# Causal attention with decay ahead of a two-layer MLP: a 32-row mask, wide transposes, and two blocks of pairs moved beside the first MLP block

## The chip, the cores and the metric

The kernel runs on one NeuronCore of a Trainium2 chip. The metric is the device time of one execution in microseconds (us), the median of several runs; less is better. TensorE (PE) multiplies matrices, VectorE (DVE), ScalarE (ACT) and GpSimd (POOL) work on elements, SyncE (SP) issues most of the transfers. Each engine takes its instructions in the order in which the program lists them.

## The reference

```python
scores = scale * np.matmul(q, k.transpose(0, 1, 3, 2))      # 8 batches, 8 heads, 576 x 64
s_pos = np.maximum(s, 0.0)
cum = np.cumsum(s_pos, axis=-1)
bias = -(cum[:, :, :, None] - cum[:, :, None, :])
scores = np.where(causal, -1000000000.0, scores + np.minimum(bias, 0.0))
attn = softmax(scores)
x = np.matmul(attn, v) -> transposed to 4608 tokens x 512
h = x @ w_in                                                 # 512 x 2048
g = h * np.clip(h + 3.0, 0.0, 6.0) / 6.0
out = g @ w_out                                              # 2048 x 512
```

The inputs and the output are float32; the kernel multiplies in float16.

## The kernel before

**Attention.** The 64 heads are taken as 32 pairs, four pairs to a batch. For each pair, `load_qk` and `load_v` bring q, k and v to SBUF in float32, in rows of 64 elements (256 bytes). `cast_qk` turns q and k to float16 on POOL, and `transpose_group` transposes them on TensorE in two halves of five and four tiles, with copies by DVE into `qkT`, whose halves are called `qT` and `kT`. There are three slots of `qkT`, `v_f`, `v_h` and `Pm`, and a pair p uses slot p % 3. From pair 10 on (`PTD`) the transposition is done by DMA (`cast_columns`, `transpose_dma`).

Rows 0 to 63 of `qT` and `kT` are q and k. Rows 64 to 67 add the decay: `kT` gets the running sum of s, split into three float16 parts (`kaug`), and `qT` gets its negative (`qaug`). A chain of DVE operations (`s8`, `c8`, `kaug`, L102 to L115) makes them for all heads. Pair 0 gets its rows from SBUF, the others from copies of `kaug` and `qaug` in DRAM (`load_aug`). Rows 68 to 127 are a coarse causal mask in steps of `GRAN` = 10 positions: a 1 in one operand meets -16384 in the other. It is copied from `amask` by ACT and DVE (`mask_rows`).

`scores_bank` multiplies one of four banks of scores, ACT takes the exponential into `Pm`, and POOL zeroes the upper triangle of the diagonal tiles (L295, four instructions a head). `attend` multiplies by v, with a column of ones that gives the row sums; DVE divides (L341, L343) into `xs`; `x_transpose` writes `xT`, the MLP's input.

**MLP.** The 4608 tokens are 9 blocks of 512. `m1(n, f)` is one of 16 column tiles of layer 1 (L408, four matmuls, then ACT's L416 and DVE's L417), `m2(n, t4, part)` a quarter of a row tile of layer 2 (L430). Weights come by casting DMAs from POOL: `load_w_in` in halves, `load_w_out` in quarters. Part p of layer 2 needs quarter p.

**Order.** The schedule is manual: an engine's order is that of the program. `att_tasks(p)` lists the steps of pair p; `att_of` groups them. The pairs 0 to 3 and the first part of pair 4 run alone. `weave` then deals attention tasks between MLP tasks in proportion to their costs: pairs 4 to 8 beside layer 1 of block 0 and the first eight tasks of layer 2, pairs 9 to 12 beside layer 1 of block 1 and the other eight, later four pairs beside each block. `loads` and `casts` within a pair's tasks issue later pairs' loads and casts; `pairs_at` and `weights_at` say which.

PSUM has eight banks: two of tag M, three of tag S, two of tag O, one of tag Y.

Of the kernel before, what the change touches and what calls it, by code (L numbers as in the profile page):

```python
# [9 lines left out]
F32 = mybir.dt.float32  # L10
# [6 lines left out]
def kernel(  # L17
# [23 lines left out]
    GRAN = 10  # L41
# [5 lines left out]
    NS = 3  # L47

# [3 lines left out]

    def bank():
        return psum.tile([128, 512], F32, tag="M", bufs=2, name="bank")

    ident_dram = nc.inline_tensor(np.eye(128, dtype=np.float16), name="ident_f16")

    gran = np.arange(SEQ) // GRAN
    rows = np.arange(60)
    amask_np = np.ones((2, 64, SEQ), dtype=np.float16)  # L60
    amask_np[0, 4:64] = gran[None, :] == rows[:, None]
    amask_np[1, 4:64] = np.where(gran[None, :] < rows[:, None], -16384.0, 0.0)
    amask_dram = nc.inline_tensor(amask_np, name="amask")

    row = np.arange(W2).reshape(NTR, 128).T % SEQ
    xaug_np = np.concatenate([amask_np[1][:, row], amask_np[0][:, row]], axis=2)
    xaug_dram = nc.inline_tensor(
        np.ascontiguousarray(xaug_np.transpose(1, 2, 0)).reshape(128, 2 * NTR * 64),
        name="xaug",
# [25 lines left out]
    amask = work.tile([128, 2, SEQ], F16, tag="amask", bufs=1)  # L95
    s_sb = work.tile([NH, SEQ], F32, tag="s0", bufs=1)
    nc.sync.dma_start(out=s_sb, in_=s.rearrange("b h t -> (b h) t"))
    nc.scalar.dma_start(out=amask[64:128], in_=amask_dram.ap().rearrange("i p t -> p i t"))
    nc.scalar.dma_start(out=ident, in_=ident_dram.ap())

# [18 lines left out]
    nc.gpsimd.memset(warm, 0.0)  # L119
    nc.gpsimd.memset(kT[:, :, W2:W2 + 64], 0.0)  # L120
    nc.gpsimd.memset(v_f[64:128, :, :, 4, :], 0.0)
    nc.gpsimd.memset(v_h[:, :, :, :, D:VW], 1.0)
    nc.gpsimd.memset(Pm[:, :, 1600:PW], 1.0)

    def mask_rows(sl, copy):
        for i, dst in enumerate((kT, qT)):
            copy(
                out=dst[64:128, sl, 0:W2].rearrange("p (h t) -> p h t", h=2),
                in_=amask[64:128, i:i + 1, :].to_broadcast([64, 2, SEQ]),
            )  # L130
# [5 lines left out]
    def load_qk(p, eng):  # L136
        b, h0 = (2 * p) // H, (2 * p) % H
        t = work.tile([128, NTR, 2, D], F32, tag="qkf", bufs=3, name=f"qkf{p}")
        for i, src in enumerate((q, k)):
            rows = src[b, h0:h0 + 2].rearrange("h s d -> (h s) d")  # L140
            eng.dma_start(  # L141
                out=t[:, :, i, :], in_=rows.rearrange("(t p) d -> p t d", p=128)
            )
        qk_f[p] = t

    def load_v(p, eng):
        b, h0 = (2 * p) // H, (2 * p) % H
        sl = p % NS
        for hh in range(2):
            eng.dma_start(  # L150
                out=v_f[:, sl, hh, 0:4, :],
                in_=v[b, h0 + hh, 0:512].rearrange("(t p) d -> p t d", p=128),
            )
        eng.dma_start(
            out=v_f[0:64, sl, :, 4, :],
# [9 lines left out]
    def cast_qk(p):  # L165
        t = work.tile([128, NTR, 2, D], F16, tag="qkh", bufs=2)
        nc.gpsimd.tensor_copy(out=t, in_=qk_f.pop(p))  # L167
        qk_h[p] = t

    xaug = cpool.tile([128, 2 * NTR, 64], F16, tag="c_xaug")  # L170

    def load_columns():
        nc.sync.dma_start(out=xaug.rearrange("p t c -> p (t c)"), in_=xaug_dram.ap())

    def copy_columns():
        for i in range(2):
            nc.vector.tensor_copy(out=xb[:, i, :, 64:128], in_=xaug)

# [47 lines left out]
    def cast_v(p):  # L226
        sl = p % NS
        copy = nc.vector.tensor_copy if p in (1, 2, 3, 4) else nc.gpsimd.tensor_copy
        copy(out=v_h[:, sl, :, :, 0:D], in_=v_f[:, sl])  # L229

    def half_bank(early):

        if early:
            return psum.tile([128, 640], F16, tag="M", bufs=2, name="pTm")
# [7 lines left out]
    def transpose_group(p, g):  # L242
        t0, t1 = ((0, 5), (5, 9))[g]
        n = (t1 - t0) * 128
        pT = half_bank(p < 5)
# [10 lines left out]


# [4 lines left out]
        (896, [(1, 256, 576), (4, 512, 576)]),  # L262
        (1280, [(2, 256, 576)]),
# [5 lines left out]
        (4, 4): 1216, (2, 2): 1280, (2, 3): 1408, (2, 4): 1536,  # L269
# [372 lines left out]
```

## Time and profile before

| | |
|---|---|
| median of 3 runs | 382.48 us (381.65 to 382.67) |
| span of the profiled execution | 378.1 us |
| busy, TensorE | 353.6 us (94%) |
| busy, VectorE / ScalarE / GpSimd | 190.8 / 210.4 / 146.4 us |
| first scores (L282) | 12.59 us |
| first matmul of layer 1 (L408) | 42.78 us |
| first matmul of layer 2 (L430) | 73.16 us |
| queue q1 (SP's transfers) | 182,536 packets, 54.52 MB, 68.2% of 16 engines |
| queue q0 (weights, from POOL) | 4.19 MB as written, 5.9% |

The span runs from the first to the last instruction of one profiled execution. A share of a queue is the time that its packets took, as a share of the span of all 16 DMA engines. A busy TensorE is not one at its peak, since matmuls overlap. In the listings, a row of the timeline gives start, duration, engine, line, operation, output and input, and in brackets how long the engine had been idle and what ended that.

### The profile page before, as it was taken

The numbers are of one execution on the slowest core, as the hardware profiler recorded it, in microseconds if no ns is written. First come the engines' busy times: TensorE is split into PE (matmuls) and PEld (weight loads), VectorE is DVE, ScalarE is ACT, GpSimd is POOL, SyncE is SP. The second block draws the span as 40 slices with busy tenths as digits, with TensorE's granted clock in tenths as the row PEclk, the third lists the DMA queues.
The fourth block names the chain that finished last, engine by engine and source line by source line (L and its number), as shares of the span: only waits on it lengthen the run. The fifth ranks groups of instructions, "written<-read, shape, count | busy, mean of one in ns | idle before, by whom it ended". The sixth has DMA issues, their size and how long they took to land.

```text
span 378.1 us, 7609 instructions
## 1 busy us (share of the span) xinstructions
PE 353.6 (94%) x2780; PEld 219.8 (58%) x2780; DVE 190.8 (50%) x329; ACT 210.4 (56%) x406; POOL 146.4 (39%) x375
## 2 busy tenths in 40 slices
PE   7766778899999999999999999999999999999995
PEld 3454455566666666666666666666666655555542
DVE  5554466875545444544444445445444554454531
ACT  4745466456866666666656666666666543443310
POOL 4365444364565444444444554454453100000000
PEclk9989699999999999999999999999999999999999
DMA  8699999945999999999999998999854001010011
GB/s 181 137 204 193 194 208 249 210 105 132 200 186 243 204 211 200 216 203 203 197 190 199 214 208 179 206 211 200 185 114 106 31 30 55 28 55 29 28 66 74
DMA packets 184621, 59.38 MB, mean 157 GB/s; under 512 B 177828, under 2 KB 178212, under 8 KB 184584
## 3 DMA queue, kind: packets, MB, share of 16 engines
q1 hardware_dynamic: 182536, 54.52, 68.2%
q0 software_dynamic: 1632, 4.19, 5.9%
q8 instruction: 22, 0.36, 0.4%
q10 hardware_dynamic: 416, 0.19, 0.2%
q14 instruction: 15, 0.12, 0.1%
HBM read 37.41 MB, written 9.73 MB: 125 GB/s over the span
## 4 chain that ended last, share of the span: by engine, by line
PE 82%; DMA 9%; DVE 3%; ACT 2%; SPq 1%; issue 1%; POOL 1%; POOLq 0%; ACTq 0%; DVEq 0%
PE bank L408 31%; PE po L430 30%; PE S L282 9%; PE O L331 7%; DMA qkf<-in_k_dram 5%; DMA v_f<-in_v_dram 3%; PE bank L430 3%; ACT Pm L290 2%; PE pT L369 1%; DMA s_sb<-in_s_dram 1%; PE bank L450 1%; SPq L141 1%; POOL t L167 1%; DVE qkT L253 1%; DVE kaug L115 0%
## 5 line engine op out<-in xcount | busy, mean ns | idle before, releaser
L416 ACT ACTIVATE trl<-bank,bias 128x512 f32<-128x512 f32 x144 | 99.5, 691 | 111.8 <-PE bank L408 110.8
L417 DVE SCALAR_TENSOR_TENSOR gT<-trl,bank 128x512 f16<-128x512 f32 x144 | 99.1, 688 | 121.8 <-ACT trl L416 121.8
L408 PE MATMUL bank<-xT,w_in 128*128 128x512 f16 x576 | 148.3, 383 | 1.3 <-DVE gT L417 1.3
L290 ACT ACTIVATE Pm<-S 128x384 f16<-128x384 f32 (+2 forms) x256 | 116.2, 505 | 32.3 <-PE S L282 30.6
L295 POOL TENSOR_SCALAR_AFFINE_SELECT Pm<-Pm 128x128 f16<-128x128 f16 (+2 forms) x256 | 79.0, 311 | 135.4 <-ACT Pm L290 126.6
L430 PE MATMUL po<-w_out_sb,gT 128*128 128x512 f16 x528 | 130.9, 379 | 0.0
L408 PEld LDWEIGHTS <-w_in 128*128 128x128 f16 x576 | 77.5, 146 | 31.6 <-issue 2.8
L430 PEld LDWEIGHTS <-gT 128*128 128x128 f16 x576 | 53.2, 98 | 51.4
L282 PE MATMUL S<-qkT 128*128 128x320 f16 (+4 forms) x448 | 70.2, 265 | 6.9 <-DVE qkT L253 2.3
L282 PEld LDWEIGHTS <-qkT 128*128 128x128 f16 x448 | 41.4, 99 | 34.2 <-DVE qkT L253 2.7
L331 PEld LDWEIGHTS <-Pm 128*128 128x128 f16 x960 | 39.1, 98 | 12.1 <-POOL Pm L295 0.4
L331 PE MATMUL O<-v_h,Pm 128*128 128x65 f16 x960 | 41.6, 195 | 0.3 <-POOL Pm L295 0.3
L343 DVE TENSOR_TENSOR xs<-O,r 128x640 f16<-128x640 f32 x32 | 26.4, 824 | 1.1
L213 POOL CAST xb<-qkf 128x1152 f16<-128x1152 f32 x22 | 25.3, 1149 | 0.0
L439 DVE TENSOR_SCALAR osb<-po 128x512 f32<-128x512 f32 x33 | 22.6, 685 | 5.0 <-PE po L430 5.0
L229 POOL CAST v_h<-v_f 128x640 f16<-128x640 f32 x28 | 20.6, 737 | 2.2 <-DMA v_f<-in_v_dram 2.2
L341 DVE RECIPROCAL r<-O 128x10 f32<-128x10 f32 x32 | 7.1, 220 | 25.6 <-PE O L331 25.4
L167 POOL CAST t<-qkf 128x1152 f16<-128x1152 f32 x10 | 11.8, 1177 | 12.2 <-DMA qkf<-in_k_dram 12.2
L238 PEld LDWEIGHTS <-t 128*128 128x128 f16 x90 | 6.3, 99 | 12.1 <-POOL t L167 8.2
L253 DVE COPY qkT<-pTm 64x640 f16<-64x640 f16 (+1 forms) x20 | 9.1, 453 | 7.8 <-PE pTm L238 7.6
L450 PE MATMUL bank<-warm 128*128 128x512 f16 x30 | 9.5, 487 | 2.2 <-POOL warm L119 1.4
L430 PE MATMUL bank<-w_out_sb,gT 128*128 128x512 f16 x48 | 11.3, 379 | 0.0
(40 smaller groups left out, 80.2 us busy)
## 6 DMA issues: line engine op xcount, KB each, us to landing
qkf<-in_q_dram SPq DMA_DIRECT2D x32, 288.0 KB, 3.6
qkf<-in_k_dram SPq DMA_DIRECT2D x32, 288.0 KB, 4.2
out_dram<-osb SPq DMA_DIRECT2D x36, 256.0 KB, 2.0
v_f<-in_v_dram SPq DMA_DIRECT2D x64, 128.0 KB, 3.6
w_in<-in_moe_w_in_dram POOLq DMA_DIRECT2D x2, 1024.0 KB, 11.0
w_out_sb<-in_moe_w_out_dram POOLq DMA_DIRECT2D x4, 512.0 KB, 8.3
v_f<-in_v_dram SPq DMA_DIRECT2D x32, 32.0 KB, 8.2
qkT<-xb SPq DMA_TRANSPOSE x22, 5.2
```

What stands on the lines that cost most here:

```text
L213: nc.gpsimd.tensor_copy(out=x.rearrange("p (i t) c -> p t i c", i=2)[:, :, :, 0:D], in_=qk_f.pop(p))
L229: copy(out=v_h[:, sl, :, :, 0:D], in_=v_f[:, sl])
L282: nc.tensor.matmul(out=S[:, c:c + hi - lo], lhsT=kT[:, sl, off + 128 * kt:off + 128 * (kt + 1)], rhs=qT[:, sl, off + lo:off + hi], start=( ...
L290: nc.scalar.activation(out=P[:, p0:p0 + n], in_=S[:, 0:n], func=AF.Exp, scale=0.125, bias=0.0)
L295: nc.gpsimd.affine_select(out=view, in_=view, pattern=pattern, compare_op=ALU.is_ge, fill=0.0, base=0, channel_multiplier=-1,)
L331: nc.tensor.matmul(out=O[:, hh, qt * VW:qt * VW + D + 1], lhsT=P[:, c:c + 128], rhs=v_h[:, sl, hh, kt, 0:D + 1], start=(qt == 0), stop=(qt ...
L343: nc.vector.tensor_tensor(out=xs.rearrange("p t h d -> p h t d"), in0=Ov[:, :, :, 0:D], in1=r.to_broadcast([128, 2, 5, D]), op=ALU.mult,)
L408: nc.tensor.matmul(out=ph, lhsT=w_in_t[f // 8][:, kc, f % 8, :], rhs=xT[:, kc, n * 512:(n + 1) * 512], start=(kc == 0), stop=(kc == KC - 1),)
L416: nc.scalar.activation(out=trl, in_=ph, func=AF.Relu, bias=bias3[:, 0:1], scale=1.0)
L417: nc.vector.scalar_tensor_tensor(out=gT[n][:, f, :], in0=trl, scalar=6.0, in1=ph, op0=ALU.min, op1=ALU.mult)
L430: nc.tensor.matmul(out=po, lhsT=gT[n][:, f, t4 * 128:(t4 + 1) * 128], rhs=w_out_sb[:, f, :], start=(f == 0), stop=(f == NF - 1),)
L439: nc.vector.tensor_scalar_mul(out=osb, in0=po, scalar1=1.0 / 6.0)
```

## The change

- The mask has 32 rows in steps of 18 (rows 68 to 99). Score matmuls read 100 rows (`KR`). The mask comes by DMA directly into `qkT`; DVE memsets write ones to rows 64 to 67 of all slots, and ones and zeros to the fixed columns of `xb`, ahead of the decay chain.
- q and k of pairs 0 and 1 (`ROWS`) are loaded in contiguous runs of nine rows per partition. Their transposes go to one tile of two banks (`transpose_rows`), and `rows_of_head` copies each head with strided reads. This pool is closed afterwards and its banks become those of tag M. Pair 0 is cast by ACT; v of pairs 0 and 1 is loaded by casting DMAs from POOL.
- A one-element copy by POOL, `hold`, waits for the end of the decay chain.
- Banks 2 and 3 of the scores are rearranged, so that three POOL instructions a head mask the diagonals.
- The order of the first two batches is written out by hand: pairs 0 to 3, then layer 1 of block 0 beside pairs 4 and 5, with three PSUM banks, then layer 2 of block 0 beside pairs 6 and 7. The first three tiles of layer 1 start with three of their four chunks. Pair 8 and what follows come after; layer 1 of block 1 has the last four tasks of layer 2 of block 0 beside it. w_in is loaded at the end of pair 0 and in pair 3, w_out in `own(5)`.

```diff
+    nc.vector.memset(qkT[64:68, :, 0:2 * W2], 1.0)
+    nc.vector.memset(xb[:, :, :, D:D + 4], 1.0)
+    nc.vector.memset(xb[:, :, :, KR:128], 0.0)
...
     def cast_qk(p):
         t = work.tile([128, NTR, 2, D], F16, tag="qkh", bufs=2)
-        nc.gpsimd.tensor_copy(out=t, in_=qk_f.pop(p))
+        if p == 0:
+            for i in range(2):
+                nc.scalar.copy(out=t[:, :, i, :], in_=qk_f[p][:, :, i, :])
+        else:
+            nc.gpsimd.tensor_copy(out=t, in_=qk_f[p])
+        qk_f.pop(p)
         qk_h[p] = t
...
+    load_v(0, nc.gpsimd)
+    load_v(1, nc.gpsimd)
...
+    def rows_of_head(p, hh):
+        for dst, r0 in ((kT, 64), (qT, 0)):
+            nc.vector.tensor_copy(
+                out=dst[0:64, p, hh * SEQ:(hh + 1) * SEQ].rearrange("d (j t) -> d j t", t=NTR),
+                in_=T_tiles[p][r0:r0 + 64, 0:W2].rearrange("d (t j) -> d j t", j=128)[
+                    :, hh * 64:(hh + 1) * 64
+                ],
+            )
...
-                lhsT=kT[:, sl, off + 128 * kt:off + 128 * (kt + 1)],
-                rhs=qT[:, sl, off + lo:off + hi],
+                lhsT=kT[0:KR, sl, off + 128 * kt:off + 128 * (kt + 1)],
+                rhs=qT[0:KR, sl, off + lo:off + hi],
...
-            if (n, t4) in ((0, 1), (8, 1), (8, 3)):
+            if (n, t4) in ((8, 1), (8, 3)):
...
+    load_qk(2, nc.sync)
     load_aug(1, nc.sync)
-    load_qk(2, nc.sync)
     load_v(2, nc.sync)
+    load_aug(2, nc.sync)
+    load_qk(3, nc.sync)
+    load_v(3, nc.sync)
...
+    def pair_of_first_batch(p):
+        s0, s1 = scores(2 * p), scores(2 * p + 1)
+        if p == 0:
+            return (
+                s0[:3] + step(transpose_rows, 1) + step(rows_of_head, 1, 0)
+                + step(rows_of_head, 1, 1) + step(single_banks) + s0[3:]
+                + s1 + step(cast_qk, 2) + step(load_w_in, 0) + att(0)
+                + step(load_aug, 3, nc.sync)
+            )
...
+    def own(p):
+        cast_qk(p)
+        if p == 5:
+            for c in range(4):
+                load_w_out(c)
+        cast_v(p)
+        load(p + 3)
...
+    def pair_of_next_batch(p):
+        s0, s1 = scores(2 * p), scores(2 * p + 1)
+        aug = step(load_aug, p + 3, nc.sync) if p + 3 < PTD else []
+        if p == 4:
+            return (
+                halves(4) + [(lambda: None, 1500)] + s0 + s1 + aug + att(8) + step(own, 5)
+            )
+        if p == 5:
+            return att(9) + halves(5) + xt(4) + [(lambda: None, 800)] + s0 + s1 + aug + att(10)
...
-    keep_warm(18)
-    cast_qk(0)
-    transpose_group(0, 0)
-    transpose_group(0, 1)
-    mask_rows(2, nc.vector.tensor_copy)
-    cast_v(0)
+    keep_warm(11)
+    transpose_rows(0)
+    rows_of_head(0, 0)
+    rows_of_head(0, 1)
+    nc.gpsimd.tensor_copy(out=hold, in_=kaug[:, 2, SEQ - 1:SEQ])
     cast_qk(1)
-    keep_warm(12)
-    for task, _ in att_of[0]:
+    load(4)
+    keep_warm(10)
+    for p in range(4):
+        for task, _ in pair_of_first_batch(p):
+            task()
+    x_transpose(2)
+    for f in range(2):
+        m1(0, f, range(3))
+    attend(7)
+    m1(0, 2, range(3))
+    x_transpose(3)
+    for f in range(3):
+        m1(0, f, range(3, 4))
+    m2_0 = m2_tasks(0)
+    m1_0 = m1_tasks(0)
+    own(4)
+    weave(pair_of_next_batch(4), m1_0[3:9])
+    weave(pair_of_next_batch(5), m1_0[9:])
+    own(6)
+    m2_0[0][0]()
+    attend(11)
+    load_columns()
+    decay_columns()
+    for task, _ in m2_0[1:4]:
         task()
+    x_transpose(5)
+    for task, _ in halves(6):
+        task()
+    m2_0[4][0]()
+    weave(att_of[1], m2_0[5:12])
+    weave(att_of[2], merged(m1_tasks(1), m2_0[12:], 1))
```

## The prediction

> **What bounds the kernel now.** I read the tenths of the page first, for where TensorE is not full.
>
> ```profile
> ## 2 busy tenths in 40 slices
> PE   7766778899999999999999999999999999999995
> ...
> PEclk9989699999999999999999999999999999999999
> DMA  8699999945999999999999998999854001010011
> ```
>
> A slice is 9.45 us. TensorE is full from slice 9 on; the eight slices before are not, and in most of those the DMA engines read 9. So the place to win time is the first 75 to 90 us, and the suspect there is the transfer of inputs. The table by stretches (span, busy us and count of each engine, granted clock, DMA share, GB/s), cut at 73.2 us, where layer 2 of block 0 begins, says how much is left to win:
>
> ```profile
> 0.00:73.20 73.20, 54.24 (x505) 35.55 (x506) 42.68 (x84) 40.45 (x78) 35.57 (x84) 0.93 0.96 196
> 73.20:121.20 48.00, 46.91 (x453) 30.96 (x453) 28.34 (x57) 30.43 (x64) 25.81 (x67) 1.00 0.85 173
> 121.20:373.70 252.50, 252.46 (x1829) 153.25 (x1826) 119.07 (x188) 139.49 (x264) 85.05 (x225) 1.00 0.68 144
> ```
>
> After 121.2 us TensorE is busy 252.46 of 252.50 us, and the waits of that stretch hold none for TensorE. The diff leaves that part's matmuls alone, so the end moves exactly as much as the moment from which TensorE is full. Third, the chain that ended last, in order of time (start, us, what), names what that moment waited for:
>
> ```profile
> 15.93 3.96 DMA qkf<-in_k_dram
> ...
> 27.48 11.71 DMA v_f<-in_v_dram
> 42.99 1.65 PE bank L408 x4
> ...
> 49.85 13.93 DMA qkf<-in_k_dram
> ...
> 73.23 0.97 PE po L430 x4
> ```
>
> Layer 1 starts at 43 us because the values of pair 4 took 11.7 us to land (both halves of w_in, issued at 26.3 and 30.8, were in flight), and layer 2 starts at 73.2 behind a key load of 13.9 us (all of w_out was in flight). Fourth, the timeline of the start (start, us, engine):
>
> ```profile
> 3.80 0.45 DVE L102 TENSOR_SCALAR s<-s_sb 64x576 f32<-64x576 f32 x1 [3.80 <-DMA s_sb<-in_s_dram]
> ...
> 7.42 1.58 DVE L115 TENSOR_TENSOR kaug<-r,kaug 64x576 f16<-64x576 f32 x1
> ...
> 12.59 0.71 PE L282 MATMUL S<-qkT 128*128 128x256 f16 x6
> ...
> 15.48 0.40 SPq L141 DMA_DIRECT2D qkf<-in_q_dram  x1
> ```
>
> The decay chain on VectorE (3.8 to 9.0) decides the first scores at 12.6: copies and the small row loads follow it. SP reaches pair 2 only at 15.5, since it queues behind the decay rows.
>
> **What the skill says.** (1) The Trainium skill, "DMA: Bandwidth & Descriptors", section "Queues, rings and completion order": each DMA engine goes round-robin between the queues that have work. The trace agrees: a quarter of w_out took 8.3 us from issue to landing, and key loads went from 4.2 (median) to 13.9 us meanwhile. (2) "VectorE: DVE Perf Modes", section "Zero memsets can be issued as uint32 (trn2)": a memset takes one cycle per element whatever the type. The trace has no large one on VectorE; on POOL, 512 f16 took 0.525 us and 192 took 0.258, about 1 ns each, which fits. (3) "SBUF — State Buffer", section "Who interferes with whom": a VectorE instruction with two SBUF inputs contends with a POOL instruction that reads SBUF. L113 took 0.75 us and L115, the same size beside a POOL cast, 1.58: it agrees.
>
> **Unit prices.** TensorE, pipelined in the chain: four matmuls of a layer 0.863 us, one attend of 15 matmuls 0.47, a head's scores 0.68, nine transposes 0.5, five 0.28. DMA: queue q1 is 182,536 packets and 68.2% of 16 engines' 378.1 us, so 22.6 ns a packet; a pair's q, k, v are 3,456 packets of 256 B, 4.9 us of all 16 engines. Queue q0 is the weights: 5.9%, 22.3 us, 5.6 for half of w_in and 2.8 for a quarter of w_out. The DMA share was 1.03 over 43 to 73 us, so these prices add up to elapsed time.
>
> **The change, part by part, against the profiled span of 378.1.**
>
> *Start, VectorE.* Three memsets stand in front of the decay chain. Per partition they write 3 x 2304 = 6,912, 36 x 4 = 144 and 36 x 28 = 1,008 elements, 8,064 in all. At one per cycle of 0.96 GHz (the page's clock) that is 8.4 us, 8.6 with starts, from 0.8 to 9.4. The chain then begins 5.6 us later; its last step loses its POOL contention (0.75 for 1.58, POOL stands in `hold`), so it ends at 13.8 in place of 9.0. Lower bound: VectorE's idle time until 3.8 hides them all, cost zero (or -0.8 by that contention). I take the page's price: first scores at about 16.5 (rows issued at once, 2.4 us to land), +3.9.
>
> *Start, the rest.* Mask copies leave ACT (4 x 1.15 us) and VectorE (2 x 0.87): on no path (ACT did them while waiting for `c8` and for scores). In their place 0.44 MB of long rows, at the 322 GB/s at which the trace moves 2304-byte packets (114 ns each), 1.4 us of DMA before anything else is wanted. The cast of pair 0 goes from POOL (1.21) to ACT (two of 576, 0.68 each as in L460), hidden by the chain. The two-bank transposes: 8 copies of 64x576 in place of 8 of 64x640 and 64x512 over two pairs; 0.46 each as L377, up to 0.74 if the stride halves the rate (0.14 fixed, from the 64x640 and 64x512 copies' 0.49 and 0.42, plus 576 at one per cycle); I take 0.6, +0.6 a pair at most, not on the path after pair 1. Values of pairs 0, 1 by casting DMAs: six issues on POOL of 0.55 to 0.83 us (L390, L383), about 4 us while POOL has nothing else, and no casts. Contiguous rows for q, k of pairs 0, 1: 256 packets of 114 ns for 2,304 of 22.6, 1.8 us for 3.3, so -1.4 a pair. Nine fewer warm matmuls lie ahead of data.
>
> *SP's queue.* The decay rows still stand ahead of pair 2: with the late chain SP issues it at about 15, as before (15.5). But then come pair 2, its rows, pair 3, and only then pair 4; and layer 1 needs only pairs 0 to 3 and half of w_in (pair 4 is now beside layer 1). From 15: pairs 2, 3 and half of w_in, 9.8 + 5.6 = 15.4, plus about 3 of pair 4 interleaved, so layer 1 begins near 34, not 43. Attention itself allows that: four pairs at about 4 us (POOL: six masks, 2.2, and two casts, 1.9) from 16.5.
>
> *Layer 1 of block 0 with pairs 4, 5.* TensorE: 16 x 0.863 + 2 x (1.36 + 0.94 + 0.5) + 0.28 = 19.7, so not before 54. The third bank and the split fourth chunk save at most the 1.3 us that L408 waited for gT.
>
> *w_out.* Its four issues stand on POOL behind the cast of pair 5. By then the DMA has moved w_in and pairs 2 to 5: 11.2 + 19.6 = 30.8 us of share from 15, so about 45. Then w_out alternates with pairs 6, 7: the four took 17 us in before (46.1 to about 63); alone-by-half they take up to 2 x 11.1 = 22. I take 19: the last quarter lands at 64, and layer 2's fourth part, which needs it, ends at 64.9. This, not TensorE's 54, is the bound.
>
> *From there to equal work.* In before, at 118.9 layer 1 of block 1 and layer 2 of block 0 are done, 24 attends and 26 heads' scores (counts of L408, L430, L331, L282 in stretches). From layer 2's start to that state the changed order has 32 x 0.863 + 13 x 0.47 + 14 x 0.68 + 4 x 0.5 + 4 x 0.28 + 1.1 (decay columns) = 47.4 us of TensorE, of which 5.0 precede 64.9. So 64.9 + 42.4 + 2.5 of stalls (the before's 45.7 us from 73.2 held as much) = 109.8: 9.1 us sooner. DMA until then: pairs 8 to 12 and some transposes keep two pairs ahead.
>
> *Other new waits and moves.* `hold` makes POOL wait for the chain's end; behind it stand the cast of pair 1 (1.15) and then the masks of pair 0, whose transposes and exps come after 16.5 anyway. The single banks wait for the copies of pair 1's transposes; behind that on TensorE stand pair 2's transposes, one bank of scores later, hidden by ACT's 2 us of exps. w_in's halves are issued (0.83 each) behind the casts of pairs 2 and before pair 3's last masks, so the first at about 20.5 and landing near 32 at half share. The rows of pair p+3 wait on SP for scores of pair p, with only loads of pairs needed 6 us or more later behind them. The mask columns (half the bytes) and decay columns move beside layer 2's first part: their copies, 12 of L205 and 4 of L207, 3.7 us of VectorE, lie beside the wait for w_out.
>
> *At nothing:* three masks per head for four (-0.13 us of POOL), K of 100, granules of 18, bank order, pair 3's divided normalisation, casts moved from VectorE to POOL: all beside a TensorE that is full, or before it beside DMA.
>
> Sum: 378.1 - 9.1 = 369.0 on the profile. The three timed runs have a median of 382.48 against this execution's span of 378.1, so 373.4.
>
> **The rivals.** *Memsets are free:* everything up to w_out comes 4.8 us earlier, the end -13.9, 368.6. For it: VectorE is idle until 3.8. Against: the price of (2). *The gain is given back:* pairs 9 to 12 stand beside 20 tasks instead of 24, 29.6 us of TensorE, 7.4 a pair, and the DMA is asked for 4.9 of loads, 3.3 for 2,304 packets of qkT's transpose and 0.7 for xT's, 8.9; if the lead of two pairs is gone, 3 to 6 us come back, 377. *Nothing is won,* DMA moves the same bytes in the same time, 382. *Slower:* POOL's queue holds w_out behind a cast that waits for pair 5's keys. If that load takes the 13.9 us seen at 49.85, w_out is issued near 54.5 and, at 21.5 us for the four, lands at 76; then 0.9 + 42.4 + 2.5 gives 121.8 for 118.9, +2.9, 385.4. It decides from a landing of w_out after 73.1. Against it: pair 5 is issued ahead of w_out and in before that slow load had all of w_out beside it. That the change does not do what it says I exclude: its copies, banks and queues are unconditional.
>
> **How the numbers follow.** Forecast 0.5, free memsets 0.27, given back 0.07, nothing 0.03, slower 0.13. Faster by over 0.3% (about 1.1 us, what a measurement can tell): 0.84; within 0.03; slower 0.13. Range: 365 (free memsets and w_out in 16 us) to 381 (most of the gain given back).
>
> **What would show it.** Right: first scores near 16.5 with VectorE's chain ending near 13.8; layer 1 near 34; last w_out near 64; TensorE full from then. First scores near 11.5 make the memset price wrong; a landing of w_out near 73 or TensorE waits for casts beside pairs 9 to 12 make the rest wrong.

## The result and the profile after

The changed kernel takes 386.75 us (median of four runs, 385.81 to 387.97) where the kernel before takes 382.38 in the same session: ratio 1.0119, 95% interval 1.0084 to 1.0154. It is slower by some 4.4 us, and the forecast was 9.1 faster. In some executions a kernel runs a per cent or more slower: the ratios below leave these out, the medians do not, and the one profile of run e14 is of such an execution and is not read.

The profiled executions are 384.5 and 378.1 us long, 6.4 apart. Both lie below their medians, by 2.2 and 4.3 (some 1.7 of each is time outside the span), so this pair of profiles overstates the gap by about 2 us. Changes of 1 us between two profiles are read with that in mind.

The tenths of the page, TensorE, its clock and the DMA engines, a slice being 9.6 us:

```profile
PE   6684799977998999999999999999999999999996
...
PEclk8678899999999999999999999999999999999999
DMA  9798978975799999999998999799944101001012
```

TensorE has a 4 in the fourth slice (29 to 38 us) and two 7s at 77 to 96 us, where before it was at 9. The clock reads 8, 6, 7, 8, 8 in the first five slices, and DMA has a hole of 7, 5, 7 in slices nine to eleven. The table by stretches (span, busy us and count of TensorE, its weight loads, VectorE, ACT and POOL, granted clock, DMA share, GB/s), cut at layer 1's start, at layer 2's fourth part, at 95 us and where TensorE is full:

```profile
0.00:41.46 41.46, 27.88 (x234) 18.19 (x235) 25.12 (x37) 17.38 (x36) 20.71 (x48) 0.76 0.95 173
41.46:71.60 30.14, 26.89 (x238) 17.10 (x236) 19.95 (x47) 17.61 (x33) 11.62 (x22) 0.99 0.91 179
71.60:95.00 23.40, 18.47 (x186) 11.47 (x186) 12.27 (x29) 10.09 (x24) 10.88 (x22) 1.00 0.72 161
95.00:125.00 30.00, 28.13 (x261) 19.07 (x261) 15.73 (x28) 21.28 (x44) 16.04 (x37) 1.00 0.97 177
125.00:380.00 255.00, 255.00 (x1856) 154.96 (x1855) 120.29 (x190) 141.93 (x270) 81.53 (x191) 1.00 0.70 146
```

From 125 us TensorE is full, as the prediction had it of the late part. All of the loss lies before that: the changed kernel has done layer 2 of block 0, layer 1 of block 1, 24 attends and 26 heads' scores at 125.9 us, the kernel before at 118.8, and from there they take 258.6 and 259.2 us to their ends. The chain that ended last (start, us, what), in three stretches: the start, the time ahead of layer 1, and layer 2's first parts:

```profile
2.31 5.82 DVE qkT L136
...
12.39 0.75 DVE kaug L154
...
13.72 3.02 DMA kaug_scratch<-kaug
16.76 0.60 SPq L199
...
25.46 5.44 SPq L178
...
30.95 1.62 SPq L187
...
33.86 0.41 SPq L199
...
34.32 1.36 DMA qkT<-qaug_scratch
...
35.81 1.17 PE S L344 x5
...
56.68 1.09 POOL t L208
...
59.32 12.26 DMA w_out_sb<-in_moe_w_out_dram
71.62 1.02 PE po L510 x4
```

First the memset of ones, then the decay chain, then SP. Then from 25.46 SP is held for 5.44 us issuing a key load (pair 4's), then issues pair 4's values, and issues only at 33.86 the decay rows (L199, L200) that pair 3's scores wait for. Last, w_out stands behind POOL's cast of pair 5, and that cast follows the last mask of pair 4. TensorE's waits in 12 to 41.5 us and in 66.6 to 95 us (in total, times, longest) say the same, and name one more:

```profile
PE S L344 <- DMA qkT<-qaug_scratch: 3.6, 1, 3.6
PE S L344 <- DVE qkT L312: 2.8, 1, 2.8
```

```profile
PE pTm L279 <- POOL t L208: 2.6, 2, 1.7
```

The last is POOL's cast of the next pair's queries and keys: transposes beside layer 2 wait for it. POOL's timeline shows the place of such a cast, pair 7's, behind the six masks of pair 6:

```profile
76.14 0.78 POOL L357 TENSOR_SCALAR_AFFINE_SELECT Pm<-Pm 128x256 f16<-128x256 f16 x2 [7.35 <-ACT Pm L352]
77.34 1.17 POOL L357 TENSOR_SCALAR_AFFINE_SELECT Pm<-Pm 128x256 f16<-128x256 f16 x3 [0.42 <-ACT Pm L352]
79.31 0.41 POOL L357 TENSOR_SCALAR_AFFINE_SELECT Pm<-Pm 128x256 f16<-128x256 f16 x1 [0.80 <-ACT Pm L352]
79.66 1.14 POOL L208 CAST t<-qkf 128x1152 f16<-128x1152 f32 x1
```

### The profile page after: what moved, and what is told of

Read it like the earlier page. It is cut to its first block, busy times and chain, and to the rows that moved or that the text cites. A ratio compares the mean times of both kernels' runs of the same rounds, so it can differ in the third digit from the quotient of the medians.

```text
span 384.5 us, 7470 instructions
## 1 busy us (share of the span) xinstructions
PE 357.1 (93%) x2771; PEld 221.0 (57%) x2771; DVE 194.1 (50%) x328; ACT 208.3 (54%) x405; POOL 140.8 (37%) x319
## 3 DMA queue, kind: packets, MB, share of 16 engines
q1 hardware_dynamic: 176040, 54.00, 67.3%
## 4 chain that ended last, share of the span: by engine, by line
PE 77%; DMA 6%; DVE 4%; SPq 3%; issue 3%; ACT 3%; POOL 2%; POOLq 0%; ACTq 0%
PE po L510 29%; PE bank L486 28%; PE S L344 10%; PE O L395 6%; DMA w_out_sb<-in_moe_w_out_dram 3%; ACT Pm L352 2%; PE bank L510 2%; DVE qkT L136 2%; DMA qkT<-xb 1%; SPq L178 1%; POOL t L208 1%; POOL Pm L357 1%; DMA kaug_scratch<-kaug 1%; SPq L187 1%; PE pT L438 1%
## 5 line engine op out<-in xcount | busy, mean ns | idle before, releaser
L496 ACT ACTIVATE trl<-bank,bias 128x512 f32<-128x512 f32 x139 | 95.8, 690 | 103.1 <-PE bank L486 100.7
L486 PE MATMUL bank<-xT,w_in 128*128 128x512 f16 x556 | 142.9, 382 | 1.8 <-DVE gT L497 1.1
L510 PE MATMUL po<-w_out_sb,gT 128*128 128x512 f16 x544 | 134.7, 379 | 0.2
L357 POOL TENSOR_SCALAR_AFFINE_SELECT Pm<-Pm 128x256 f16<-128x256 f16 (+1 forms) x192 | 70.2, 369 | 156.5 <-ACT Pm L352 151.4
L344 PE MATMUL S<-qkT 100*128 100x320 f16 (+4 forms) x448 | 73.9, 272 | 11.2 <-DMA qkT<-qaug_scratch 3.6
L344 PEld LDWEIGHTS <-qkT 100*128 100x128 f16 x448 | 41.5, 101 | 44.1 <-issue 4.1
L410 DVE TENSOR_TENSOR xs<-O,r 128x640 f16<-128x640 f32 (+1 forms) x33 | 26.5, 804 | 1.3 <-DVE r L409 0.2
L409 DVE RECIPROCAL r<-O 128x10 f32<-128x10 f32 (+1 forms) x33 | 7.2, 218 | 28.6 <-PE O L395 28.5
L294 DVE COPY qkT<-pTm 64x640 f16<-64x640 f16 (+1 forms) x20 | 9.1, 453 | 12.7 <-PE pTm L279 12.5
L530 PE MATMUL pw<-warm 128*128 128x512 f16 x21 | 7.5, 527 | 1.4 <-POOL warm L212 1.4
L279 PE MATMUL pTm<-ident,t 128*128 128x128 f16 x45 | 4.2, 238 | 3.9 <-POOL t L208 3.9
```

Source lines behind the costliest of these rows:

```text
L344: nc.tensor.matmul(out=S[:, c:c + hi - lo], lhsT=kT[0:KR, sl, off + 128 * kt:off + 128 * (kt + 1)], rhs=qT[0:KR, sl, off + lo:off + hi], s ...
L357: nc.gpsimd.affine_select(out=view, in_=view, pattern=pattern, compare_op=ALU.is_ge, fill=0.0, base=0, channel_multiplier=-1,)
L410: nc.vector.tensor_tensor(out=x_tiles[p].rearrange("p t h d -> p h t d")[:, h0:hh + 1], in0=Ov[:, :, :, 0:D], in1=r.to_broadcast([128, hh ...
L486: nc.tensor.matmul(out=ph, lhsT=w_in_t[f // 8][:, kc, f % 8, :], rhs=xT[:, kc, n * 512:(n + 1) * 512], start=(kc == 0), stop=(kc == KC - 1),)
L496: nc.scalar.activation(out=trl, in_=ph, func=AF.Relu, bias=bias3[:, 0:1], scale=1.0)
L510: nc.tensor.matmul(out=po, lhsT=gT[n][:, f, t4 * 128:(t4 + 1) * 128], rhs=w_out_sb[:, f, :], start=(f == 0), stop=(f == NF - 1),)
```

## The experiments

All ratios are to the kernel before, timed beside each. Unless said otherwise the edit is made on the changed kernel, and the times read off a trace ("first scores", "layer 1") are starts on TensorE, in us.

| run | edit | median us | ratio, 95% interval | first scores | layer 1 |
|---|---|---|---|---|---|
| - | the change itself | 386.75 | 1.0119 (1.0084 to 1.0154) | 15.0 | 41.3 |
| e1 | ones by DMA | 386.50 | 1.0150 (1.0088 to 1.0212) | 15.2 | 40.5 |
| e2 | pair 4's loads behind pair 3's rows | 382.71 | 1.0034 (1.0002 to 1.0067) | 15.0 | 37.7 |
| e3 | casts ahead of masks | 383.24 | 1.0056 (1.0033 to 1.0078) | 15.0 | 41.7 |
| e4 | even weave | 387.89 | 1.0186 (1.0146 to 1.0226) | 15.0 | 41.1 |
| e5 | e2 and e3 | 378.94 | 0.9931 (0.9909 to 0.9953) | 15.0 | 35.7 |
| e6 | w_out earlier | 385.60 | 1.0128 (1.0069 to 1.0187) | 15.0 | 40.3 |
| e7 | free start | 386.69 | 1.0141 (1.0079 to 1.0203) | 10.8 | 38.9 |
| e8 | e5, e6 and e7 | 382.15 | 1.0013 (0.9984 to 1.0042) | 11.1 | 40.7 |
| e9 | kernel before with the memset | 385.90 | 1.0079 (1.0058 to 1.0100) | 19.1 | 49.2 |
| e10 | e5, e7, w_in later | 380.63 | 0.9935 (0.9904 to 0.9965) | 10.7 | 37.7 |
| e12 | e5 and 20 warm-ups | 378.06 | 0.9871 (0.9835 to 0.9908) | 15.0 | 35.8 |
| e13 | split ones | 387.79 | 1.0110 (1.0068 to 1.0152) | 13.4 | 40.6 |
| e14 | e5 and e13 | 382.91 | 0.9972 (0.9945 to 1.0000) | - | - |
| e15 | e5, plain loads of values | 379.26 | 0.9907 (0.9875 to 0.9939) | 15.3 | 36.1 |
| e16 | e5 again | 379.51 | 0.9910 (0.9877 to 0.9944) | 15.0 | 35.7 |
| e17 | e14, w_in two masks later | 379.12 | 0.9951 (0.9925 to 0.9978) | 13.7 | 38.2 |
| e18 | e17 and 20 warm-ups | 378.21 | 0.9913 (0.9887 to 0.9940) | 13.4 | 35.2 |

**The order on SP (e2) and on POOL (e3), and both (e5, e16).**

```diff
-                + step(load_aug, 3, nc.sync)
+                + step(load_aug, 3, nc.sync) + step(load, 4)
...
     cast_qk(1)
-    load(4)
```

> The decay rows of pair 3 are issued on SP ahead of the loads of pair 4. Theory SP (the rows stood behind pair 4's keys, whose issue was held for 5.4 us, and TensorE waited 3.6 us for them): that wait goes, layer 1 starts near 37.5 instead of 41.3, the end comes 2 to 4 us sooner, about 383.5. Rival DMA: the wait reappears at pair 3's values or at w_in, and the end moves by under 1 us.

```diff
         if p == 6:
-    return s0 + s1 + aug + step(own, 7) + att(12) + halves(7)
+    return step(own, 7) + s0 + s1 + aug + att(12) + halves(7)
...
-    s0 + att(13) + s1 + xt(6) + step(own, 8) + att(14) + halves(8)
+    step(own, 8) + s0 + att(13) + s1 + xt(6) + att(14) + halves(8)
```

> The casts and loads of pairs 7 and 8 stand ahead of the scores of pairs 6 and 7, so on POOL ahead of their masks. Theory POOL (between 72 and 95 us TensorE waits for casts that stand behind masks): the waits of 1.7 and 0.8 us for POOL go, the end comes 2 to 3 us sooner, about 384. Rival thin work (too few MLP tasks lie beside pairs 6 to 8, so attention's own chain of exp and mask sets the pace): the waits move to exp and copies, the end moves by under 1 us. A third outcome is a loss, if the casts hold the masks back while they wait for keys.

> Both orders of the two runs before that gained: pair 3's rows ahead of pair 4's loads, and the casts of pairs 7, 8 ahead of the masks. Theory two waits (each is a wait of its own in a different stage, so they add): -3.0 and -2.4 us, about 5.4 us under the changed kernel, so about 1 us under the kernel before. Rival one bound (a transfer, w_out's last quarter, stands behind both): they do not add, and the end is 3 us under the changed kernel, 1.5 above before.

> The two reorderings that gained, once more, on the same chip as the three others, as their common base: ratio 0.993 within 0.003, layer 1 near 35.7. If the granted clock of the first 41 us alone made the gain of twenty warm-up matmuls (0.9871), this base shows a clock near 0.83 there and a ratio above 0.990; if it comes out at 0.988 or under, that gain was scatter between chips.

Against the changed kernel's 1.0119, e2 gives back 0.0085 (3.2 us), e3 0.0063 (2.4 us), and both 0.0188 and 0.0209 (7.2 and 8.0 us, the second on another chip). Each alone is just clear of the changed kernel's interval, so its size is known only roughly; both together are well clear, and that they give more than the sum of 5.6 is within the intervals. So the two orders alone turn a kernel that is 1.2% slower into one that is 0.7 to 0.9% faster. SP's timeline in e16 shows the first mechanism:

```profile
23.86 1.05 SPq L199 DMA_DIRECT2D qkT<-kaug_scratch  x1
24.96 0.78 SPq L200 DMA_DIRECT2D qkT<-qaug_scratch  x1
25.83 0.53 SPq L178 DMA_DIRECT2D qkf<-in_q_dram  x1
26.41 5.22 SPq L178 DMA_DIRECT2D qkf<-in_k_dram  x1
```

Pair 3's rows are issued at 23.86, 10 us sooner, and pair 4's key issue still holds SP for 5.22 us, now with nothing urgent behind it. TensorE's wait for rows is gone from the list of 12 to 42 us, and layer 1 begins at 35.7. (In e2's profile, 383.8 us long, 2.2 us of it are left, and layer 1 begins at 37.7.) In e3 pair 7's cast starts at 69.15 in place of 79.66, and the wait pTm for POOL's cast is gone from 66.6 to 95 us.

**The ones (e1, e7, e9, e13, and e8, e10, e14, e17 with other edits).** e9 puts the memset alone into the kernel before:

```diff
+    nc.vector.memset(qkT[64:68, :, 0:2 * W2], 1.0)
     s8 = work.tile([NH, SEQ], F32, tag="s1", bufs=1)
```

> The kernel before, with the one memset of 6,912 ones per partition put ahead of its decay chain and nothing else changed (the rows it fills are written over later). If the start sets the end in the kernel before, as the prediction had it, the chain ends about 4 us later, the first scores move from 12.6 to about 16, and the end is 2 to 4 us later (ratio 1.005 to 1.010). The rival: the start has slack behind the loads in flight, and a chain that is 4 us late is made up by the time layer 1 begins; then the ratio is within 0.003 of 1.

It costs 3.0 us of the median. The timelines of SP, the kernel before and then e9, show one thing that moved by as much, the load of pair 1's decay rows, 3.07 us later; pairs 2 and 3 are issued behind it:

```profile
14.65 0.44 SPq L162 DMA_DIRECT2D qkT<-kaug_scratch  x1
```

```profile
17.72 0.44 SPq L164 DMA_DIRECT2D qkT<-kaug_scratch  x1
```

In that one profiled execution the first scores came 6.5 us later and the span was 7.1 longer, more than the medians carry, so that this load sets the cost is likely and not shown.

On the changed kernel the ones were freed in two ways. In e1 four rows of ones stand in front of the mask's 32 in its transfer (first diff), and e7 also moves the other slots' mask rows behind pair 0's decay rows, and pair 1's values behind its cast (second diff):

```diff
-            out=qkT[68:100, sl0:sl1, 0:2 * W2],
+            out=qkT[64:100, sl0:sl1, 0:2 * W2],
...
-    nc.vector.memset(qkT[64:68, :, 0:2 * W2], 1.0)
-    nc.vector.memset(xb[:, :, :, D:D + 4], 1.0)
-    nc.vector.memset(xb[:, :, :, KR:128], 0.0)
...
     keep_warm(10)
+    nc.vector.memset(xb[:, :, :, D:D + 4], 1.0)
+    nc.vector.memset(xb[:, :, :, KR:128], 0.0)
```

```diff
-    load_v(1, nc.gpsimd)
...
     load_qk(1, nc.sync)
-    mask_rows(1, 3, nc.sync)
     cast_qk(0)
...
+    mask_rows(1, 3, nc.sync)
     load_qk(2, nc.sync)
     load_aug(1, nc.sync)
...
     cast_qk(1)
+    load_v(1, nc.gpsimd)
```

> The ones come with the mask's DMA (36 rows in place of 32) and the memsets of xb stand behind pair 1's first copies, so nothing stands ahead of the decay chain. Theory chain (the memset of 7.3 us ahead of the chain moved everything behind it): the chain ends near 8.3 instead of 13.1, first scores near 11 instead of 15.0, and the end comes 3 to 5 us sooner, about 382.5. Rival DMA (the order of transfers sets the first 72 us, engines wait for it anyway): first scores come sooner but layer 1 still starts near 41, and the end moves by under 1 us.

> The ones come with the mask's DMA as in the run with ones by DMA, and besides the masks of slots 1 and 2 and the values of pair 1 are transferred behind pair 0's decay rows. Theory two guards (the memset and the backlog of transfers ahead of pair 0's rows each held the first scores at 15, so undoing one showed nothing): first scores at 11 to 12, and the end 2 to 4 us sooner than the changed kernel. Rival: the first scores come sooner, but pair 2 and the rows of pairs 1 and 2 do not, and the end moves by under 1 us.

In e13 only the first slot's ones stay ahead of the chain:

```diff
-    nc.vector.memset(qkT[64:68, :, 0:2 * W2], 1.0)
+    nc.vector.memset(qkT[64:68, 0:1, 0:2 * W2], 1.0)
-    nc.vector.memset(xb[:, :, :, D:D + 4], 1.0)
-    nc.vector.memset(xb[:, :, :, KR:128], 0.0)
...
+    keep_warm(11)
+    transpose_rows(0)
+    rows_of_head(0, 0)
+    rows_of_head(0, 1)
+    nc.vector.memset(qkT[64:68, 1:NS, 0:2 * W2], 1.0)
+    nc.vector.memset(xb[:, :, :, D:D + 4], 1.0)
+    nc.vector.memset(xb[:, :, :, KR:128], 0.0)
     load_qk(2, nc.sync)
     load_aug(1, nc.sync)
...
-    keep_warm(11)
-    transpose_rows(0)
-    rows_of_head(0, 0)
-    rows_of_head(0, 1)
```

> The changed kernel with its memset of ones split: VectorE writes only the first slot's ones (2,304 per partition, 2.4 us, inside its wait for s) ahead of the decay chain; the other two slots' ones and the two memsets of xb follow pair 0's copies. No transfer is added or moved up. If the memsets cost what they delay, the chain ends near 8.5, the first scores come near 11.5 in place of 15.0, and the end moves 2 to 4 us down: ratio to the kernel before 1.001 to 1.007. The rival: the transfers ahead of layer 1 set its start, the freed time is waited for at pair 3's rows and keys, and the ratio stays at 1.012 within 0.003.

> The same split together with the two reorderings that gained (pair 4's loads behind pair 3's rows, casts ahead of masks). If the start still counts once the wait for pair 3's rows is gone, layer 1 begins 2 to 4 us ahead of 35.7 and the ratio is 0.983 to 0.989. The rival: DMA is full from the first loads to layer 1 and bytes set its start, so the ratio is that of the two reorderings alone, 0.993 within 0.003.

In e1 the decay chain ends at 8.6 in place of 13.1, but TensorE waits 4.8 us for pair 0's decay rows, which SP issues from 8.3 to 14.0, between waits for transfers. e7 brings the first scores to 10.8 and e13 to 13.4, in place of 15.0. Neither moves the end beyond the noise, and with the two orders mended the split (e14, 0.9972) does no better than its base (0.9910 in e16, 0.9931 in e5). Two reasons can be read from the traces. The first is the order of two bulk loads. In e13 POOL reaches w_in's first half at 19.50, ahead of pair 3's keys on SP (20.35; in the changed kernel w_in is at 21.49, behind the keys at 20.74). From e13's timeline and chain:

```profile
19.50 0.78 POOL L451 DMA_DIRECT2D w_in<-in_moe_w_in_dram  x1
```

```profile
20.35 10.60 DMA qkf<-in_k_dram
31.07 1.15 POOL t L206
```

The keys take 10.60 us, and TensorE waits 6.7 us for their cast. In e16, with w_in at 21.50 and the keys at 20.75, that cast starts at 26.47. Over the runs the keys take longer the sooner w_in comes: 9.85 and 8.0 us with it 0.12 and 0.42 us behind them (e8, e17), at most 5.7 with it 0.5 to 0.75 behind (e18, e16). Putting w_in later is e10 (behind pair 3's cast, with e5's orders and e7's start; first diff) and e17 (two masks later, on e14; second diff):

```diff
-                + s1 + step(cast_qk, 2) + step(load_w_in, 0) + att(0)
+                + s1 + step(cast_qk, 2) + att(0)
...
-                + step(cast_qk, 3) + att(2) + step(load_aug, 4, nc.sync)
+                + step(cast_qk, 3) + step(load_w_in, 0) + att(2) + step(load_aug, 4, nc.sync)
```

```diff
-                + s1 + step(cast_qk, 2) + step(load_w_in, 0) + att(0)
+                + s1 + step(cast_qk, 2) + att(0)
...
-                s0[:3] + halves(2)[:1] + s0[3:] + halves(2)[1:] + att(1) + s1
+                s0[:3] + step(load_w_in, 0) + halves(2)[:1] + s0[3:] + halves(2)[1:] + att(1) + s1
```

> The freed start (ones from a mask DMA, other rows behind pair 0's) with the two reorderings that gained (pair 4's loads behind pair 3's rows, casts ahead of masks), and the first half of w_in issued one pair later, behind the cast of pair 3. If the freed start was lost before because w_in then stood ahead of pair 3's keys, pair 3's keys land within about 6 us, layer 1 begins by 35 and the time is at or under that of the two reorderings alone (378.9, ratio 0.993 or less, to 0.985 if the 4 us of the start arrive whole). The rival: the input bytes set the start of layer 1 whatever the order, w_in then lands too late instead, and the time is as with everything moved (382, ratio 1.0).

> The split memset with the two reorderings, and the first half of w_in issued two masks later on POOL, behind the first three banks of pair 1's scores, so that it again follows pair 3's keys (20.4 us on SP) as it does in the changed kernel. If the order of w_in and these keys is what took the freed start back, the keys land within 6 us, layer 1 begins at 34 or before, and the ratio is 0.983 to 0.990. The rival: the bytes ahead of layer 1 set its start, layer 1 begins at 35.7 or later, with a wait for w_in, and the ratio is 0.991 or more.

Neither beats the base. In e10 w_in comes at 27.0 and layer 1 waits 2.1 us for it. In e17 it is at 20.78, 0.4 us behind the keys, and they still take 8 us. The second reason holds for all of them: SP's load of pair 1's decay rows stands at 16.76 in the changed kernel and at 16.40 (e7), 17.42 (e8), 16.86 (e10), 16.70 (e13) and 16.71 (e17), since it now waits for the mask transfer (3.0 to 4.3 us in e7, e8 and e10) or for the other slots' ones (1.4 and 1.1 us in e13 and e17). TensorE's longest wait of 12 to 42 us in e7 shows what became of the early scores:

```profile
PE S L343 <- DMA qkT<-kaug_scratch: 5.1, 1, 5.1
```

It waits there for pair 1's rows (5.5 us in e8 and in e10). And pair 3's keys, which SP issues later still, were issued at 20.1 to 21.1 in every run. The first scores were freed, and SP was not. A start that frees SP too was not tried, so that it would pay is not shown.

**All moved (e8) and w_out alone (e6).**

```diff
         cast_qk(p)
-        if p == 5:
-            for c in range(4):
-                load_w_out(c)
         cast_v(p)
+        if p == 4:
+            for c in range(4):
+                load_w_out(c)
         load(p + 3)
```

> Only w_out moves: its four issues go from behind the cast of pair 5's keys to behind the cast of pair 4's values, some 15 us earlier. Theory w_out (its late landing at 71.6 us takes the gain): the last quarter lands before 62 and the end comes over 3 us sooner. Rival (TensorE reaches the last quarter's matmuls at about 71 anyway, because layer 1 began late and pairs 4, 5 take their time): less than 1 us, and a loss if it delays the keys of pairs 5 and 6.

> The free start, pair 3's rows first, casts first and w_out early together. If the waits are of different stages, their gains add: 3.0 + 2.4 + 2 to 4 from the start and 1 from w_out, 8 to 10 us under the changed kernel, 4 to 6 under before, about 377. If the DMA engines are the bound before 72 us, it is not under the run with rows and casts alone.

e6 gains nothing, though w_out stood on the chain at 71.6: it is issued at 42.7 and leaves the chain, but layer 2 begins at 65.9 (66.6 in the changed kernel) and the waits for POOL's casts stay at 2.6 us. In e8 pair 3's keys (21.07) and w_in (21.19) are in flight together, the keys take 9.85 us and TensorE waits 5.4 for their cast, more than the 3.1 us by which e8 is behind e5. w_out is on the chain again in e16 (53.99 to 67.85, and TensorE waits 1.7 us for it); e5 with only w_out moved was not run.

**Even weave (e4).**

```diff
-    weave(pair_of_next_batch(4), m1_0[3:9])
-    weave(pair_of_next_batch(5), m1_0[9:])
-    own(6)
...
-    weave(att_of[1], m2_0[5:12])
-    weave(att_of[2], merged(m1_tasks(1), m2_0[12:], 1))
+    mid = pair_of_next_batch(4) + pair_of_next_batch(5) + step(own, 6) + att(11)
+    mid += [(lambda: (load_columns(), decay_columns()), 640)] + xt(5) + halves(6)
+    weave(mid + att_of[1], m1_0[3:] + m2_0[:8])
+    weave(att_of[2], merged(m1_tasks(1), m2_0[8:], 2))
```

> Pairs 4 to 8 in one list, dealt evenly beside the last 13 tasks of layer 1 and the first 8 of layer 2, and the other 8 beside layer 1 of block 1, as the kernel before has it; the rest of the change stays. Theory thin work (8 tasks of layer 2 beside pairs 6, 7 and part of 8 leave TensorE to wait about 5 us in 72 to 95 us, and it waits again beside the 20 tasks of pairs 9 to 12): the end comes 4 to 7 us sooner, about 381. Rival early start (the loss lies before layer 1, and the order after it only passes it on): the end moves by under 1.5 us.

It is no faster, and its interval overlaps the changed kernel's. In the changed kernel TensorE waits once beside pairs 9 to 12 for a pair transposed by DMA, 1.1 us at 121.5, which the kernel before does not have; e4 does not have it either. So thin work beside pairs 9 to 12 is not what made the loss, unless the even deal costs as much elsewhere.

**Casting loads (e11, e15).**

```diff
-    load_v(0, nc.gpsimd)
-    load_v(1, nc.gpsimd)
...
     load_qk(0, nc.sync)
+    load_v(0, nc.sync)
     load_qk(1, nc.sync)
+    load_v(1, nc.sync)
...
     load_qk(3, nc.sync)
+    cast_v(0)
+    cast_v(1)
     load_v(3, nc.sync)
```

> The two reorderings that gained, with the values of pairs 0 and 1 loaded as float32 by SP and cast on POOL in place of casting DMAs. If the 2,400 extra packets of the casting DMAs took about 45 ns each, 6.5 us of all 16 engines fall to about 2.2 and pair 2's loads and rows land 3 to 4 us sooner: ratio 0.985 to 0.990 against the kernel before (the two reorderings alone: 0.993). The rival: POOL, with two more casts of 1.1 us, becomes late for pair 0's masks or for the cast of pair 2, and the time is the same or up to 2 us longer.

> The two reorderings that gained, with the values of pairs 0 and 1 loaded as float32 by SP and cast on POOL ahead of the cast of pair 1, in place of casting DMAs. If the casting transfers' small packets took about 45 ns each (6.5 us of all 16 engines for two pairs), the time falls by 1 to 3 us against the two reorderings alone (ratio 0.985 to 0.990). The rival: the freed engine time lies where VectorE's chain decides, or POOL's two casts delay the cast of pair 1, and the ratio is 0.993 or up to 0.998.

The diff is e15's, on e5. e11 (389.21 us, 1.0172, 1.0133 to 1.0211) had pair 0's cast after pair 3's load of the same slot in the program, so pair 0 was computed with pair 3's values and waited for them: it says nothing of the question. e15 has it in order. The DMA share of the first 12 us falls from 1.07 (e16) to 0.71, and the time stays, 0.9907 to 0.9910. The casting loads' price does not reach the end; in both runs the first scores come at 15.0 to 15.3.

**The clock (e12 on e5, e18 on e17).**

```diff
-    keep_warm(10)
+    keep_warm(20)
```

> The two reorderings that gained, with 20 warm-up matmuls in place of 10 ahead of pair 0's scores. If the low granted clock of the first 41 us (0.76) comes from TensorE standing idle between 12 and 15 us, the clock of 12 to 41 us rises above 0.9, and the time falls by 1 to 3 us against the two reorderings alone (378.9). The rival: TensorE waits for data there, so a faster clock only lengthens its waits, and the time stays at 378.9 within 1 us.

> The same with 20 warm-up matmuls in place of 10 ahead of pair 0's scores. If the clock before 41 us is worth something where nothing else is late, its mean there rises from about 0.7 to above 0.85 and the ratio falls by 0.003 or more, to 0.980 to 0.986; the rival, TensorE waits for data there anyway or the warm-ups hold pair 0's scores up, has it within 0.002 of the run without them.

The stretch 12 to 41.5 us in e16, then in e12 (columns as above; the third number from the end is the granted clock):

```profile
12.00:41.50 29.50, 21.58 (x235) 15.45 (x236) 17.00 (x34) 15.26 (x35) 15.93 (x33) 0.77 0.91 174
```

```profile
12.00:41.50 29.50, 20.93 (x245) 14.51 (x244) 16.95 (x34) 15.09 (x35) 16.06 (x33) 0.94 0.92 172
```

The clock rises from 0.77 to 0.94. The two pairs of runs gain 0.0039 and 0.0038 (e12 against e16, e18 against e17), 1.5 us, but the intervals of each pair overlap, and the traces do not tie the gain to the clock. Layer 1 begins at 35.8 in e12 and 35.7 in e16 (and at 35.7 in e5, with a clock of 0.83), layer 2 at 61.4 and 61.3: before layer 2 nothing is won, as the rival of e12 had it. The two profiles part at w_out's last quarter, which lands at 66.3 and 67.85. In e18 layer 1 does begin 3.0 us sooner than in e17, but there pair 3's keys took at most 5.4 us in place of 8.0. So the clock followed the warm-ups, and what it is worth stays open. e12 has the lowest ratio of all, 1.3% under the kernel before.

## Why the prediction was wrong, by its own steps

*Start, VectorE.* The price was right and its reach was not settled. The memset ran from 0.8 to 8.13 us, 7.3 us for 6,912 elements; one cycle each, as the Trainium skill's "VectorE: DVE Perf Modes", section "Zero memsets can be issued as uint32 (trn2)", has it, makes an estimate of 7.2 at that page's clock. The row shows 5.82, since it starts at 2.31 after 1.5 us of "issue". In e13 the row of 4,608 ones has 3.90 us after 1.01 of "issue", 4.9 together, where the same estimate is 4.8. The chain ended at 13.1 (predicted 13.8) and the first scores came at 15.0 (16.5, from 12.6). The zero memset took 0.48 us for 1,008 f16, as uint32, where the sum charged one cycle per f16. On the kernel before the same memset costs 3.0 us (e9), so the rival that it is free fails there; what it costs the changed kernel stays open, since no run freed SP.

*SP's queue: the step that failed first.* The prediction said that the rows of pair p+3 "wait on SP for scores of pair p, with only loads of pairs needed 6 us or more later behind them". It looked at what is behind the rows, not at what is ahead: `load(4)` stands ahead of pair 3's rows, and its key issue held SP 5.44 us. Layer 1 began at 41.3, not 34. With that order mended it began at 37.7 (e2) and 35.7 (e5, e16), so the rest of the step, the bytes to layer 1, was nearly right. Cost: 3.2 us by e2, roughly.

*Casts behind masks: the step that was missing.* The prediction has no term for where POOL casts the queries and keys of pairs 7 and 8. (Its "casts moved from VectorE to POOL", entered at nothing, are those of the values.) Those casts are POOL's in both kernels. In the kernel before each stands at the head of the pair ahead of it, before that pair's masks; the order written by hand puts each behind six masks, and TensorE, which the prediction had as full there, waited for them: 2.6 us in the trace, 2.4 us of the median (e3), 7 to 8 with the order on SP.

*w_out.* Predicted issue at 45 behind pair 5's cast, landing at 64; measured 57.7 and 71.6. Pair 5's cast stands behind pair 4's masks, and these came late, as layer 1 did by 7 us. The four quarters took 13.9 us in place of 19: by luck, the landing was late by 7.6 us and not by 12.7. It was still before 73.1, the slower rival's threshold, and e6 shows that the end does not hang on w_out alone.

*From there to equal work: two terms mis-sized.* The changed kernel from layer 2's start to the same counts, then the kernel before over its own stretch:

```profile
66.63:125.90 59.27, 52.38 (x506) 34.03 (x506) 32.69 (x72) 32.91 (x70) 29.61 (x64) 1.00 0.88 174
```

```profile
73.20:118.90 45.70, 44.61 (x427) 29.61 (x427) 27.59 (x56) 28.93 (x61) 24.34 (x63) 1.00 0.84 171
```

The counts of the sum were right, its prices were not: TensorE was busy for 52.4 us where the sum has 47.4. It idled for 6.9 us, 2.6 of them for POOL's casts and 1.1 for the pair transposed by DMA, the rest in short waits for exponentials, masks and copies. The 2.5 us of stalls were taken from the kernel before, which idled for only 1.1 of its 45.7: there, too, part of what was taken for stalls was work.

*The clock.* "Nine fewer warm matmuls lie ahead of data" entered them at nothing. The clock of the first 41 us fell to 0.76 (0.91 before, same stretch). Whether that cost time is not shown (e12, e18).

*The sum.* Against the profile the forecast was 369.0 and the result 384.5, 15.5 us more. In the prediction's terms: layer 2's fourth part ended at 72.6 and not at 64.9 (7.7), the work from there was 46.5 us and not 42.4 (4.1), idle time 6.8 and not 2.5 (4.3), and the rest was 0.6 shorter. With the landing alone wrong its sum would still have come out 1.5 us faster than the kernel before (71.6 + 0.9 + 42.4 + 2.5 = 117.4 for 118.9). The two orders act on the first and the third term. In e12, which has both mended and stands at -4.9 (0.0129 of 382.9), layer 2's fourth part ends at 67.3, the work is 46.2 and the idle time 3.6: what is left of the miss is the work's price, 3.8 us, w_out's landing, 2.4, and 1.1 of waits. How much of the landing the memset holds stays open.

*The rivals.* The change was slower. The rival on that side had one thing right, w_out held on POOL behind pair 5's cast (issued at 57.7, near its 54.5), but the cast waited for masks and not for a slow load of keys. "The gain is given back" named a lost lead of the transposed pairs: that came to one wait of 1.1 us, not 3 to 6.

## What to carry to other kernels

When loads are moved earlier in a queue, list what is ahead of each small transfer that someone waits for: a bulk issue ahead of it can hold the queue while other bulk loads are in flight. Here two small rows behind one key load cost about 3 us. When an order is written anew, find the place of each piece of work among its engine's other work: a cast behind six masks is late even on an engine that is idle two thirds of the time. Check unit prices against the busy time of a whole stretch of the old kernel before taking what is left over for stalls. And a start that was freed on one engine gained nothing here while the queue that issues the next loads was not freed as well.

## What the runs showed of the hardware

A key issue on SP mostly took 0.6 us. Pair 4's, where it follows half of w_in (by 3.4 to 7.6 us), took 3.0 to 6.5 us in every trace read but e13's, where SP was held for 8.0 us one step earlier, at pair 3's values. In e10, which issues w_in only at 27.01, pair 4's keys and then pair 5's:

```profile
25.14 0.61 SPq L178 DMA_DIRECT2D qkf<-in_k_dram  x1
```

```profile
29.43 3.23 SPq L178 DMA_DIRECT2D qkf<-in_k_dram  x1
```

So pair 4's is quick ahead of w_in, and 5.44 us long 4.0 us behind it in the changed kernel. That loads of two queues slow each other agrees with the Trainium skill's "DMA: Bandwidth & Descriptors", section "Queues, rings and completion order", as the prediction used it: w_in 0.85 us ahead of a pair's keys (e13) made them 10.60 us, 0.75 us behind them (e16) no more than 5.7. The casting loads of values moved 2,400 more packets for 1.7 points of 16 engines' span (7.6% for 5.9% on that queue, 6.5 us), about 43 ns each, twice the 22.6 of the plain queue; this did not reach the end (e15). A copy from PSUM of 64x576 f16 with 128 elements between neighbours took 0.78 us (3.10 for four), where the prediction's contiguous row of 576 has 0.46; the first scores stood behind two of them.
